# A decode kernel of two attention and two FFN layers: another plan of heads, more held K and V, whole-array zero matmuls

## The chip, the cores and the metric

The kernel runs on one core of a Trainium2 chip. The metric is device time in microseconds (us), the median over executions. The core has five engines with programs of their own: TensorE (PE; weight loads are listed as PEld), VectorE (DVE), ScalarE (ACT), GpSimd (POOL) and SyncE (SP), which here issues all loads. They order their work by semaphores. The load stream runs on 16 DMA engines.

## The reference

Four tokens (batch 4, one position each, D = 448) go through attention, FFN, attention, FFN. Both attention layers use the same weights and the same caches, and both FFNs the same weights.

```python
def _A_ref(x, k_cache, v_cache, wq, wo):      # Hq 16, Hkv 8, Sk 8192, Dh 256
    W = min(4096, max(256, Sk // 4))          # 2048: the last 2048 positions
    q = (x @ wq) ...                          # (4, 16, 1, 256)
    k = jnp.repeat(k_cache[:, :, Sk - W:, :], rep, axis=1)
    v = jnp.repeat(v_cache[:, :, Sk - W:, :], rep, axis=1)
    p = _softmax(einsum("bhqd,bhkd->bhqk", q, k) * (Dh ** -0.5), axis=-1)
    o = einsum("bhqk,bhkd->bhqd", p, v)
    return o ... @ wo
def _B_ref(x, w_gate, w_up, w_down):          # F = 1792
    return (_silu(x @ w_gate) * (x @ w_up)) @ w_down

x = x + _A_ref(_layernorm(x), k_cache, v_cache, wq, wo)
x = x + _B_ref(_layernorm(x), w_gate, w_up, w_down)
x = x + _A_ref(_layernorm(x), k_cache, v_cache, wq, wo)
x = x + _B_ref(_layernorm(x), w_gate, w_up, w_down)
```

For each token, layer and KV head there is a K matrix and a V matrix of 2048 x 256 in bf16, 1 MiB each: 4 x 2 x 8 = 64 uses of a K and 64 of a V. The second layer reads the same matrices as the first.

## The kernel before

**A head** is written as three digits: token, layer, KV head. Head 103 is token 1, layer 0, KV head 3; 113 is the same cache in the second layer. Tokens are independent of one another, so token 0 runs ahead and its second layer overlaps with the first layers of the others. What ties a token's layers together is a chain: the last head of the layer, the output projection, residual, norm, FFN, norm and the new q.

**Buffers.** The tile `half` has 27 slots of 512 KB (NPOOL, HALF). A K or V matrix takes two of them. K is loaded with 16 positions of 256 values per partition, 8 in each half, so that a half has rows of 4 KB. A head of layer 0 that is among the last KEEP_K[t] (or KEEP_V[t]) of its token isn't given back after layer 0: its slots stay taken until layer 1 has used them, and that head isn't loaded again.

**A softmax group** (function `group`) works on one head or on two heads at once ("002+001" in PLAN). Its steps, by line: K half loads (L855), a 32x32 block transpose of each half on DVE (L860), V half loads (L870), the masked query `qe` on POOL (L899), the scores on PE (L894, 32 matmuls of 128 columns for one head and 32 of 256 for two), the row maximum on DVE (L907), its spread over the partitions by two matmuls (L912, L915) and a DVE maximum (L921), exp on ACT (L925), the turn of the probabilities on PE (L938) with a copy on ACT (L947), their sums (L955 on PE, L960 on DVE, the power -1 on POOL, L982), the V product on PE (L969, 8 matmuls for each half), the merge of its two parts (L984 on ACT, L986 on DVE, L992 on PE) and the scaling into `oT` (L1002). Then the output projection adds into the PSUM bank A, as rows (L1022) or, for the heads that end a layer, as columns (L1014). A `stage` of PLAN (a string) is a list of groups whose projections stand together.

**A token's chain**: `rows` (L766, L768, L776, L780) and `residual` (L784) read bank A, `norm` (L551 to L577), then an FFN, `norm` again, and `qproj` (L610 to L646). The FFN exists in two forms: `ffn_row` (L672, tokens in rows, used for the tokens in ROWF) and `ffn` (L726, L753, weights stationary, as many moving columns as there are tokens). A token whose second attention layer is done waits and shares the next token's FFN.

**The order.** Every step is an `Op` in a `Graph`, numbered as it is made. SEQ_PE, SEQ_DVE, SEQ_ACT, SEQ_POOL and SEQ_SP give each engine's program as a list of those numbers, written out by hand of a planner. SLOTS gives the slot of each load in SyncE's order. A load waits until the last PE step that used its slot (`rel`) is done: scores for a K half, the V product for a V half. SyncE issues in order, so a load that waits holds back all behind it. `schedule` estimates start times from each step's duration; they set no order, but which waits can be left out (`_place_waits`).

**Zero matmuls.** In SEQ_PE "w" stands for a matmul of 128 rows and 128 columns of zeros with 512 moving columns into bank A, which adds nothing (L1100), and "q" for the same in four quarters of 32 columns (L1106). 46 are whole, 22 in quarters. `_fill` places waits between them and the steps of other engines on bank A.

Of the kernel before, what the change touches and what calls it, by code (L numbers as in the profile page):

```python
# [20 lines left out]

# [7 lines left out]
FAR_DUR = 0.35  # L29
KEEP_K = (5, 5, 4, 5)  # L30
KEEP_V = (5, 5, 5, 3)


KLEAD = 2.0
KTAIL = 0.1
VLAG = 1.4
SLEAD = -3.4
FR = 8.0
FRD = 9.0
WOR = -5.1  # L40
CROSS = 20
# [4 lines left out]
TRP = 1  # L46
LAND = 1.5
DSTART = 2.1
ROWF = (0, 1)
PLAN = (  # L50
# [4 lines left out]
)  # L55
SEQ_PE = (
# [25 lines left out]
).split()  # L82
SEQ_DVE = (
# [64 lines left out]
).split()  # L148
MMV = 0.034
FAR = 1e30  # L150
FILLD = 0.43
TAIL = {"pe": 0.2, "dve": 0.12, "act": 0.15, "pool": 0.1, "sp": 0.05}

PE, DVE, SCA, POOL, SP = "pe", "dve", "act", "pool", "sp"
# [1022 lines left out]
```

## Time and profile before

| | |
|---|---|
| median of 3 runs | 302.62 us (302.06 to 303.54) |
| span of the profiled execution | 302.5 us |
| read from HBM | 107.58 MB |
| loads: K halves, V halves | 90 and 92 of 512 KB |
| weights: wq, wo, FFN | 3 x 1 MB + 512 KB; 8 x 448 KB; 2 x 1344 KB + 2 x 224 KB + 1568 KB |

The page gives no time of the profiled execution other than its span, from the first to the last instruction. In the profile, busy slices are tenths of 40 equal parts of the span; PEclk is the TensorE clock that was granted, in tenths of full speed. In groups of instructions, "xN" is their count, then busy us in all, mean ns of one, then the idle time of the engine ahead of them and what ended it. Matmuls overlap, so a mean of one is longer than the distance between two. "q" behind an engine's name is its sequencer, which is where loads are issued.

### The profile page before, as it was taken

The numbers are of one execution on the slowest core, as the hardware profiler recorded it, in microseconds if no ns is written. First come the engines' busy times: TensorE is split into PE (matmuls) and PEld (weight loads), VectorE is DVE, ScalarE is ACT, GpSimd is POOL, SyncE is SP. The second block draws the span as 40 slices with busy tenths as digits, with TensorE's granted clock in tenths as the row PEclk, the third lists the DMA queues.
The fourth block names the chain that finished last, engine by engine and source line by source line (L and its number), as shares of the span: only waits on it lengthen the run. The fifth ranks groups of instructions, "written<-read, shape, count | busy, mean of one in ns | idle before, by whom it ended". The sixth has DMA issues, their size and how long they took to land.

```text
span 302.5 us, 11333 instructions
## 1 busy us (share of the span) xinstructions
PE 237.7 (79%) x4962; PEld 140.3 (46%) x4962; DVE 200.8 (66%) x622; ACT 68.7 (23%) x203; POOL 86.3 (29%) x233
## 2 busy tenths in 40 slices
PE   0575598578977887888878869889898898987875
PEld 0322144134433554553445546664565456554554
DVE  7527484428567798966688778788666757675352
ACT  0030011111213323222231323312322121143130
POOL 1521013020412233233323423412126044133232
PEclk9999579855768579657795975855756575589795
DMA  7999999999999999999999999999899997999300
GB/s 284 404 400 400 409 410 404 401 403 402 397 408 384 392 405 408 381 368 401 373 406 403 360 386 366 399 411 353 327 380 395 413 391 303 310 328 408 146 2 3
DMA packets 31921, 108.32 MB, mean 358 GB/s; under 512 B 3192, under 2 KB 7296, under 8 KB 31488
## 3 DMA queue, kind: packets, MB, share of 16 engines
q1 hardware_dynamic: 31872, 107.60, 91.9%
q8 instruction: 39, 0.64, 0.8%
q14 instruction: 10, 0.08, 0.1%
HBM read 107.58 MB, written 0.00 MB: 356 GB/s over the span
## 4 chain that ended last, share of the span: by engine, by line
PE 24%; DMA 15%; DVE 8%; issue 4%; ACT 2%; POOL 0%; SPq 0%
DMA half<-in_A_v_cache_dram 8%; DMA half<-in_A_k_cache_dram 7%; PE Y L969 6%; PE S L894 5%; DVE half L860 3%; PE Z L726 3%; PE Z L753 2%; PE A L1022 2%; PE Y L938 1%; DVE oh L986 1%; PE S L912 1%; PE A L1106 1%; PE A L1014 1%; PE Y L992 1%; PE Y L955 1%
## 5 line engine op out<-in xcount | busy, mean ns | idle before, releaser
L860 DVE STREAM_TRANSPOSE half<-half 128x1024 uint32<-128x1024 uint32 x90 | 110.6, 1235 | 14.7 <-DMA half<-in_A_k_cache_dram 14.2
L969 PE MATMUL Y<-half,pT 128*4 128x256 bf16 (+1 forms) x1024 | 61.3, 341 | 15.6 <-DMA half<-in_A_v_cache_dram 11.6
L982 POOL TENSOR_TENSOR small<-small 128x2 f32<-128x2 f32 (+1 forms) x58 | 42.3, 735 | 74.1 <-DVE small L960 72.7
L894 PE MATMUL S<-half,qe 128*8 128x128 bf16 (+1 forms) x1856 | 53.2, 273 | 6.1 <-DVE half L860 2.7
L894 PEld LDWEIGHTS S<-half,qe 128*8 128x8 bf16 x1856 | 38.8, 102 | 16.1 <-DVE half L860 5.9
L925 ACT ACTIVATE praw<-S,small 104x128 bf16<-104x128 f32 (+1 forms) x58 | 21.8, 376 | 72.0 <-DVE small L921 60.5
L986 DVE SCALAR_TENSOR_TENSOR oh<-oh,small,Y 128x256 bf16<-128x256 bf16 x58 | 27.2, 468 | 14.0 <-ACT oh L984 13.6
L984 ACT ACTIVATE oh<-Y 128x256 bf16<-128x256 f32 x58 | 22.2, 382 | 61.1 <-PE Y L969 43.9
L899 POOL TENSOR_TENSOR qe<-qc,tiny 128x64 bf16<-128x64 bf16 x64 | 18.2, 292 | 62.4 <-PE S L894 50.1
L969 PEld LDWEIGHTS Y<-half,pT 128*4 128x4 bf16 (+1 forms) x1024 | 20.7, 92 | 30.9 <-DMA half<-in_A_v_cache_dram 13.6
L907 DVE TENSOR_REDUCE tiny<-S 104x1 bf16<-104x128 f32 (+1 forms) x58 | 16.8, 292 | 10.0 <-PE S L894 10.0
L947 ACT ACTIVATE pT<-Y 128x64 bf16<-128x64 f32 (+1 forms) x58 | 13.5, 232 | 34.1 <-PE Y L938 27.1
L938 PE MATMUL Y<-sel,praw 104*64 104x32 bf16 x208 | 13.8, 206 | 6.9 <-DVE oT L1002 2.8
L960 DVE TENSOR_REDUCE small<-Y 128x2 f32<-128x32 f32 (+1 forms) x58 | 10.7, 185 | 12.1 <-PE Y L955 11.5
L1002 DVE TENSOR_TENSOR oT<-Y,small 128x4 bf16<-128x4 f32 (+1 forms) x62 | 9.5, 159 | 12.1 <-PE Y L992 5.8
L1022 PE MATMUL A<-wo_sb,oT 128*4 128x448 bf16 x148 | 16.4, 446 | 1.1 <-DVE oT L1002 1.0
L1100 PE MATMUL A<-identb,small 128*128 128x512 bf16 x46 | 16.2, 456 | 0.1
L921 DVE TENSOR_REDUCE small<-S 104x1 f32<-104x32 f32 x58 | 10.3, 181 | 8.2 <-PE S L915 7.9
L912 PE MATMUL S<-small,identb 104*104 104x32 bf16 x58 | 13.5, 235 | 2.8 <-DVE tiny L907 2.6
L992 PE MATMUL Y<-tiny,oh 128*128 128x2 bf16 (+1 forms) x116 | 11.8, 171 | 4.4 <-DVE oh L986 3.9
L992 PEld LDWEIGHTS Y<-tiny,oh 128*128 128x128 bf16 x116 | 7.2, 104 | 15.7 <-DVE oh L986 9.4
L610 PE MATMUL Z<-wq_sb,xn 128*4 128x512 bf16 x120 | 13.9, 601 | 0.8 <-DVE st L563 0.8
(134 smaller groups left out, 276.7 us busy)
## 6 DMA issues: line engine op xcount, KB each, us to landing
half<-in_A_v_cache_dram SPq DMA_DIRECT2D x92, 512.0 KB, 7.8
half<-in_A_k_cache_dram SPq DMA_DIRECT2D x90, 512.0 KB, 7.8
wo_sb<-in_A_wo_dram SPq DMA_DIRECT2D x8, 448.0 KB, 13.7
wq_sb<-in_A_wq_dram SPq DMA_DIRECT2D x3, 1024.0 KB, 7.5
wd_sb<-in_B_w_down_dram SPq DMA_DIRECT2D x1, 1568.0 KB, 20.2
wg_sb<-in_B_w_gate_dram SPq DMA_DIRECT2D x1, 1344.0 KB, 15.9
wu_sb<-in_B_w_up_dram SPq DMA_DIRECT2D x1, 1344.0 KB, 17.2
wq_sb<-in_A_wq_dram SPq DMA_DIRECT2D x1, 512.0 KB, 5.4
```

What stands on the lines that cost most here:

```text
L860: return e.transpose(a, a)
L894: last = e.matmul(Sb[s_][qd:qd + 8, c0:c0 + rhs.free_size()], lhsT=qe[q_][:, P, ce, :, :].rearrange("p a n -> p (a n)"), rhs=rhs, start=(c ...
L899: g.op(POOL, 0.25, pos - SLEAD - 1, lambda e, P=P, t=t, kvh=kvh: e.tensor_tensor(qe[q_][:, P, :, :, :], qc[t][:, kvh, :, :].unsqueeze(2).b ...
L907: g.op(DVE, (0.23, 0.36)[n - 1], pos, lambda e: e.tensor_reduce(pmax[s_][0:R, :], Sb[s_][0:R, 0:N], AX.X, ALU.max), r=(f"s{s_}",), w=(f"pm ...
L925: return e.activation(praw[0:R, 0:128 * n].rearrange("p (g r l) -> p g r l", g=2 * n, l=2), Sb[s_][0:R, 0:128 * n].rearrange("p (l g r) -> ...
L938: last = e.matmul(Yb[p_][64 * h:64 * h + 64, c0:c0 + (48 if n == 2 else 32)], lhsT=praw[0:R, 64 * gg:64 * gg + 64], rhs=w, start=(gg == 0) ...
L969: last = e.matmul(Yb[p_][32 * gg:32 * gg + M, 256:512], lhsT=pT[pt][:, gg, 2 * a + hv, 4 * P:4 * P + M] if n == 2 else p1[:, gg % 2, 2 * a ...
L982: g.op(POOL, 0.69, pos, lambda e: e.tensor_tensor(ri[p_][:, 0:2 * n], rs[p_][:, 0:2 * n], expo[:, 1:1 + 2 * n], op=ALU.pow), r=(f"rs{p_}", ...
L984: g.op(SCA, 0.34, pos, lambda e: e.activation(oh[:, :], Yb[p_][:, 256:512], ACT.Copy), r=(f"y{p_}",), w=("oh",), bank=(f"Y{p_}",))
L986: g.op(DVE, 0.43, pos, lambda e: e.scalar_tensor_tensor(out=oh[:, :], in0=oh[:, :], scalar=lomask[:, 0:1], in1=Yb[p_][:, 256:512], op0=ALU ...
L992: last = e.matmul(Yb[p_][:, 2 * n * dh:2 * n * dh + 2 * n], lhsT=oh[:, :].rearrange("p (m e) -> p e m", e=2)[:, dh, :], rhs=osel[:, 0:2 * ...
L1022: last = e.matmul(Ab[32 * k:32 * k + B, 0:D], lhsT=oT[oi][:, k % 2, k // 2, :], rhs=wo_sb[:, 4 * kvh + k, :], start=False, stop=False, ski ...
```

## The change

Operations of the arithmetic stay as they are; what changes is which heads go together, what is held, how K is loaded, and all orders.

- PLAN has 40 stages with 49 groups in place of 32 with 58: 15 pairs and 34 single heads (6 and 52 before). In six pairs, written with "&", the scores are two steps (`scores(e, Ps)`), one for each head, so that the first doesn't wait for the second K.
- KEEP_K is (6, 5, 4, 7) for (5, 5, 4, 5), KEEP_V (5, 5, 4, 4) for (5, 5, 5, 3): 40 matrices for 37. ROWF is (1, 2) for (0, 1).
- WHOLE names ten heads whose K is one transfer of 1 MB into two neighbouring slots. Heads 315 and 317 in it are held ones, so eight such loads are issued, beside 68 K halves and 92 V halves.
- SyncE's order begins with x, wq and all eight wo, then K; the FFN weights stand in one block behind V of head 007.
- SEQ_PE has 294 whole zero matmuls and none in quarters. "w7" stands between the 6th and the 7th step of other engines on bank A (counted from 0 in the order in which they are made) and waits for the 6th; the 7th waits for the last of them.
- K halves are placed so that their distance in slots never needs two matmuls for one (`keys`).
- In `ffn`, each matmul has its n token columns repeated 32 // n times; the results are read once.
- A PSUM bank's waits go by owner: a step waits for the steps of the engine that had the bank before.
- Step durations come from a table, DUR, and no longer stand in the calls.

```diff
-KEEP_K = (5, 5, 4, 5)
-KEEP_V = (5, 5, 5, 3)
-ROWF = (0, 1)
+KEEP_K = (6, 5, 4, 7)
+KEEP_V = (5, 5, 4, 4)
+ROWF = (1, 2)
 PLAN = (
-    "000", "002+001", "004 005", "006", "003 007", "101", "100 102", "013", "015", "016 106 105", "017", "103",
-    "104 014 107", "201 011 012 202", "010", "200", "116 206 117 207", "114 113 203", "204+115 205", "306", "111 301",
-    "110 112 302", "213 215 305", "303 217+307", "214+304 300", "212", "216 211", "210", "312+314", "315 311",
-    "313+317", "316 310",
+    "000 001", "004 006", "005", "002 003", "007", "101", "100", "102", "014", "013", "016&015", "017+107", "106",
+    "105", "104+103", "012 201+202 011", "204", "010 117+200", "114 113", "115&206", "203", "116", "207+205",
+    "112&111", "110", "302&303", "300 215", "213", "304+216", "307", "306", "301&217", "305", "212", "210",
+    "214 316+314", "311&315", "317+310", "313+211", "312",
 )
+WHOLE = (
+    "000 001 104 111 112 205 207 312 315 317"
+)
...
+            for x in s.split():
+                if x[0] == "w":
+                    o, k = Op(len(self.ops), PE, "fw", filler), max(int(x[1:]), 1)
+                    o.deps[self.writer["identb"]] = True
+                    o.deps[inA[max(k, 1) - 1]] = True
+                    if k < len(inA):
+                        inA[k].deps[o] = True
...
         for b in bank:
-            last = self.banks.setdefault(b, {})
-            for e, d in last.items():
-                if e != eng:
-                    self._dep(o, d, True)
-            last[eng] = o
+            owner, now, before = self.banks.get(b, (eng, [], []))
+            if owner != eng:
+                owner, now, before = eng, [], now
+            for d in before:
+                self._dep(o, d, True)
+            self.banks[b] = (owner, now + [o], before)
...
-                        last = e.matmul((Zb, Z2)[gi][:, n * fc:n * fc + n], lhsT=lhsT, rhs=rhs,
+                        last = e.matmul(block((Zb, Z2)[gi], fc), lhsT=lhsT, rhs=more(rhs),
...
+                    if f"{t}{layer}{kvh}" in WHOLE.split():
+                        g.dma(1 << 20, lambda e, kc=kc, ksrc=ksrc: e.dma_start(
+                            kv[:, HALF * kc[0][0]:HALF * kc[0][0] + 2 * HALF], ksrc[:, :]), None, w=tuple(kk), cells=tuple(kc),
+                            run=8192)
...
+            parts = [(P,) for P in range(n)] if split else [tuple(range(n))]
+            for Ps in parts:
+                kw = dict(acc=(f"s{s_}",)) if Ps[0] else dict(w=(f"s{s_}",))
+                o = g.op(PE, "sch" if split else f"sc{n}", lambda e, Ps=Ps: scores(e, Ps),
+                         r=tuple(k for P in Ps for k in kks[P]) + tuple(f"qe{q_}_{P}" for P in Ps), bank=(f"S{s_}",), **kw)
+                o.rel = tuple(c for P in Ps if free_k[P] for c in kcs[P])
...
+        def filler(e):
+            return e.matmul(Ab[:, 0:512], lhsT=zero[:, 0:1].broadcast_to([128, 128]),
+                            rhs=identb[:, :].unsqueeze(1).broadcast_to([128, 4, 128]), start=False, stop=False,
+                            skip_group_check=True)
```

The new program of TensorE from the first to the second head's projection shows how the zero matmuls stand ("w1" each; sc scores, sp spread, tu turn, to sums, pv V product, fl flip, op projection; the head behind):

```
qsel w1 x38 sc000 w1 x3 sp000 w1 x4 sc001 tu000 w1 to000 sp001 w1 x4 sc004 tu001 pv000 to001 sp004 w1 x2 pv000
sc006 tu004 sp006 to004 fl000 w1 x6 op000 tu006 pv001 sc005 pv001 sp005 to006 w1 x3 fl001 w1 x5 op001 ...
```

More of the change, by code (lines that the diff above doesn't have):

```diff
@@ L172, in __init__ @@
         self.dval = 0
-        self.cell = None
-        self.mate = None
-        self.pairs = ()
-        self.rel = ()
-        self.bank = ()
+        self.cells = self.rel = self.bank = ()
         self.inc = False
@@ L183 @@
 class Graph:
-    filler = None
     tag = None
@@ L240, in _count, with schedule @@
         o.dval = self.dcount[sem]
-    def schedule(self, npool):
-        self.real = len(self.ops)
-        seq = {PE: SEQ_PE, DVE: SEQ_DVE, SCA: SEQ_ACT, POOL: SEQ_POOL, SP: SEQ_SP}
-        order = {e: [self.ops[int(x)] for x in s if x[0] not in "wq"] for e, s in seq.items()}
-        assert sum(map(len, order.values())) == len(self.ops) == len({o for s in order.values() for o in s})
-        loads = [o for o in order[SP] if o.cell is not None]
-        last = {id(c): o for o in self.ops for c in o.rel}
-        held = [None] * npool
-        for o, s in zip(loads, map(int, SLOTS)):
-            o.cell.append(s)
-            self._count(o, f"h{s}")
-            if held[s] is not None:
-                o.deps[last[id(held[s].cell)]] = True
-            held[s] = o
-        for o in self.ops:
-            o.succ = [d for d in o.deps]
+    def schedule(self, npool, filler):
+        real = len(self.ops)
+        inA = [o for o in self.ops if o.eng != PE and "A" in o.bank]
+        order = {}
+        for e, s in ((PE, SEQ_PE), (DVE, SEQ_DVE), (SCA, SEQ_ACT), (POOL, SEQ_POOL), (SP, SEQ_SP)):
+            order[e] = []
+            for x in s.split():
[5 more added lines that the diff above has]
+                        inA[k].deps[o] = True
+                    self.ops.append(o)
+                else:
+                    o = self.ops[int(x)]
+                order[e].append(o)
+        assert sum(map(len, order.values())) == len(self.ops) == len({o.i for s in order.values() for o in s})
+        last = {id(c): o for o in self.ops[:real] for c in o.rel}
+        held = [None] * npool
+        slots = iter(SLOTS.split())
+        for o in order[SP]:
+            if o.cells:
+                s0 = int(next(slots))
+                for s, cell in enumerate(o.cells, s0):
+                    cell.append(s)
+                    if held[s] is not None:
+                        o.deps[last[id(held[s])]] = True
+                    held[s] = cell
+                self._count(o, f"h{s0}")
@@ L259, in schedule @@
         free, at = {e: 0.0 for e in order}, {e: 0 for e in order}
-        done, chan, n = set(), 1.0, 0
+        done, n = set(), 0
         while n < len(self.ops):
-            go = [e for e in order if at[e] < len(order[e]) and all(d in done for d in order[e][at[e]].succ)]
+            go = [e for e in order if at[e] < len(order[e]) and all(d.i in done for d in order[e][at[e]].deps)]
             assert go, "the order does not complete"
@@ L544, in vec @@
-        def vec(rank, emit, r, w, dur=0.16, bank=()):
-            g.op(DVE, dur, rank, emit, r=r, w=w, bank=bank)
-        def norm(t, rank, x):
+                load(3 * 458752, wsb[:, 0:3 * FF].rearrange("p (c n) -> p c n", c=3),
+                     src[0:384, :].rearrange("(c p) n -> p c n", p=128), nm + "a", 3584)
+                load(229376, wsb[:, 3 * FF:], src[384:448, :].rearrange("r (h c) -> (r h) c", h=2), nm + "b", 1792)
+            load(1605632, wd_sb[:, :, :], B_w_down.rearrange("(c p) n -> p c n", p=128), "wd", 896)
@@ L902, in group @@
                     r=(f"qc{t}_{kvh}",) + tuple(f"qmask{a}" for a in range(4)), w=(f"qe{q_}_{P}",))
-            o = g.op(PE, (0.87, 1.72)[n - 1], pos - SLEAD, scores, r=tuple(k for kk in kks for k in kk) + tuple(f"qe{q_}_{P}" for P in range(n)),
-                     w=(f"s{s_}",), bank=(f"S{s_}",))
-            o.rel = tuple(c for kc, fr in zip(kcs, free_k) if fr for c in kc)
-            o.pairs = tuple(kcs)
-            g.op(DVE, (0.23, 0.36)[n - 1], pos, lambda e: e.tensor_reduce(
+            parts = [(P,) for P in range(n)] if split else [tuple(range(n))]
[4 more added lines that the diff above has]
+                o.rel = tuple(c for P in Ps if free_k[P] for c in kcs[P])
+            g.op(DVE, f"max{n}", lambda e: e.tensor_reduce(
                 pmax[s_][0:R, :], Sb[s_][0:R, 0:N], AX.X, ALU.max),
@@ L958, in total @@
                 return last
-            g.op(PE, 0.06 * n, pos, total, r=(f"pT{pt}", "onesb"), w=(f"ysum{p_}",), bank=(f"Y{p_}",))
-            g.op(DVE, 0.2, pos, lambda e: e.tensor_reduce(
+            g.op(PE, f"tot{n}", total, r=(f"pT{pt}", "onesb"), w=(f"ysum{p_}",), bank=(f"Y{p_}",))
+            g.op(DVE, f"sum{n}", lambda e: e.tensor_reduce(
                 rs[p_][:, 0:2 * n].rearrange("p (P n) -> p P n", n=2), sums.rearrange("p k P n -> p P n k"), AX.X, ALU.add),
@@ L1034, in build @@
         gi, oc, waiting, wo_in = 0, 0, [], []
-        for si, heads in enumerate(plan()):
+        for si, (heads, splits) in enumerate(zip(plan(), plan_splits())):
             where = {}
-            for batch in heads:
+            for batch, split in zip(heads, splits):
                 members, outs = [], []
```

474 lines of the change are left out of this document (214 added, 260 removed), and 165 rows, old and new, of tables (SEQ_ACT, SEQ_DVE, SEQ_PE, SEQ_POOL).

## The prediction

> **What bounds the kernel now.** I read the page first, then the busy time by stage, then what the DMA queue waits for, then the chain at the end. The page says that the load stream is the nearest thing to a bound:
>
> ```profile
> span 302.5 us, 11333 instructions
> PE 237.7 (79%) x4962; PEld 140.3 (46%) x4962; DVE 200.8 (66%) x622; ACT 68.7 (23%) x203; POOL 86.3 (29%) x233
> ...
> PEclk9999579855768579657795975855756575589795
> DMA  7999999999999999999999999999899997999300
> ...
> HBM read 107.58 MB, written 0.00 MB: 356 GB/s over the span
> ```
>
> The DMA engines are busy in all but the last three slices, yet TensorE is busy for 79% of the span too, at a granted clock that swings between 0.5 and 1. The stages tell the two apart (columns: window, length, busy us and count of PE, PEld, DVE, ACT, POOL, granted clock, DMA share, GB/s):
>
> ```profile
> 0.00:2.30 2.30, 0.00 (x0) 0.00 (x0) 1.26 (x11) 0.00 (x0) 0.81 (x9) 1.00 0.35 46
> ...
> 12.00:75.00 63.00, 45.04 (x648) 19.66 (x648) 33.80 (x75) 9.68 (x25) 12.12 (x30) 0.79 1.03 403
> 75.00:230.00 155.00, 131.19 (x2906) 80.13 (x2904) 116.46 (x330) 41.43 (x126) 47.96 (x129) 0.71 1.00 385
> 230.00:255.00 25.00, 22.68 (x484) 13.85 (x476) 16.26 (x47) 6.48 (x20) 9.31 (x25) 0.57 1.02 402
> 255.00:282.50 27.50, 22.00 (x547) 13.86 (x548) 17.61 (x56) 6.96 (x20) 8.24 (x22) 0.79 0.89 328
> 282.50:302.50 20.00, 14.71 (x388) 11.16 (x380) 8.12 (x43) 4.19 (x13) 6.05 (x14) 0.70 0.03 9
> ```
>
> 403 GB/s is the rate of a stage in which the queue never runs dry. Against it the middle loses 155 x (1 - 385/403) = 6.9 us and the stage from 255 loses 27.5 x (1 - 328/403) = 5.1 us. So of 302.5 us about 270.5 are bytes at full rate, 12 are stalls of the load stream, and 20 come after the last load. The stalls are waits for buffers, which TensorE frees (the SyncE queue's own waits: who, for whom, us in total, times, longest; last, the K loads' time to landing):
>
> ```profile
> SPq L855 <- PE Y L969: 29.8, 13, 6.9
> SPq L870 <- PE S L894: 17.8, 13, 3.5
> SPq L870 <- PE S L915: 16.5, 8, 4.8
> SPq L870 <- PE Y L992: 14.0, 5, 4.5
> DMA to landing us min/median/max: 3.9/7.8/18.0
> ```
>
> Most of these waits cost nothing, since halves are still queued while SyncE waits (median 7.8 us to landing). A half takes 0.524 MB / 403 GB/s = 1.3 us of transfer; the shortest landing is 3.9 us, so about 2.6 us of it is fixed. A buffer freed more than 2.6 us before the queue runs dry costs nothing.
>
> **The change, part by part.** The sum is made against the profiled execution's own span, 302.5 us; the median of the runs is 302.62, so what lies around the span is taken as 0.1 us.
>
> *Fewer bytes.* The lists KEEP_K and KEEP_V add up to 40 held matrices against 37. 182 halves become 176 (160 half transfers and 8 whole ones), 6 x 0.524 = 3.15 MB less: at 403 GB/s **-7.8 us**. It is nothing if the end is set by TensorE throughout; -8.2 at the 385 of the middle. Six DVE transposes go with it.
>
> *Whole K.* Of the ten names in WHOLE, 315 and 317 are among the seven K held for token 3, so eight transfers with 8-KB rows are issued, not ten. The nearest row is the stretch in which the wq weights, also 8-KB rows, load:
>
> ```profile
> 5.00:10.00 5.00, 0.98 (x7) 0.78 (x7) 4.21 (x38) 0.00 (x0) 0.09 (x1) 1.00 1.02 425
> ```
>
> 8 x 1.05 MB at 425 instead of 403 is -1.1 us; the other bound is 0. One window of weights is thin, and wq3's 4-KB rows are among them, so I take **-0.5**.
>
> *The zero matmuls.* There were 46 whole (L1100) and 22 in quarters (L1106); now 294 whole ones, counted off the order: 45 before the first scores, 64 more up to the scores of head 101, 47 up to token 0's FFN down product, 110 up to the scores of 212, 28 behind. Their price and that of the work around them depends on the clock (timeline: start, length, what, count):
>
> ```profile
> 21.04 0.41 PE L641 MATMUL Z<-wide,identb 128*32 128x128 bf16 x16
> 22.73 0.65 PE L894 MATMUL S<-half,qe 128*8 128x128 bf16 x32 [0.74 <-POOL qe L899]
> 26.58 1.67 PE L1100 MATMUL A<-identb,small 128*128 128x512 bf16 x7
> 33.35 0.60 PE L969 MATMUL Y<-half,pT 128*4 128x256 bf16 x8 [1.95 <-DMA half<-in_A_v_cache_dram]
> 36.64 3.17 PE L1100 MATMUL A<-identb,small 128*128 128x512 bf16 x7
> 61.88 0.54 PE L1022 MATMUL A<-wo_sb,oT 128*4 128x448 bf16 x4
> 70.27 1.02 PE L894 MATMUL S<-half,qe 128*8 128x128 bf16 x32 [0.17 <-DVE half L860]
> 278.27 0.39 PE L969 MATMUL Y<-half,pT 128*4 128x256 bf16 x8
> 282.29 0.36 PE L1022 MATMUL A<-wo_sb,oT 128*4 128x448 bf16 x4
> ```
>
> So a zero matmul costs 1.67/7 = 0.24 us at full clock and 3.17/7 = 0.45 at half; a head's scores 0.65 or 1.02, half a V product 0.39 or 0.60, a row projection 0.36 or 0.54. TensorE runs in program order, so what matters is whether released work stands behind them. In the opening, q is ready at about 21.5 us; 38 zero matmuls put the first scores at 21.5 + 9.1 = 30.6, where before they ran at 22.7. Nothing waits for that: the wo weights now all go ahead of K, and the first K, after 8.4 MB, cannot land before about 24 nor be transposed before 26.5. From there to the scores of 101 there are 64 zero matmuls (15.4 us), eight heads' scores (5.2), eleven V halves (4.3), five projections (1.8) and some thirty small matmuls at 0.2 (6, an estimate; L912 below takes 0.235): 32.7 us, so 63.3. The first load that needs this is the second half of V007, which reuses a buffer that the scores of 101 free, with all FFN weights behind it on SyncE. Up to there 26.7 MB are queued, 68.7 us at 403 GB/s with a start at 2.3 (the first row of the stages); less the 2.6 fixed, the issue must happen by 66.1. There are 3 us to spare at full clock: **+0.5**, and with all of it at half clock 21.5 + 17.1 + 28.8 + 25 = 92.4, 26 us late. Those are the bounds, 0 and +26. I stay near 0 because TensorE has no gap in this stretch, and the clock held in the trace until a gap came (stages of TensorE alone: busy us and count, granted clock, DMA share, GB/s):
>
> ```profile
> 30.00:32.00 2.00, 0.53 (x8) 0.75 1.03 404
> 36.00:38.00 2.00, 1.84 (x8) 0.50 1.05 416
> 40.00:41.00 1.00, 1.00 (x26) 0.50 1.04 414
> 41.00:42.00 1.00, 1.00 (x14) 0.88 1.06 422
> ```
>
> Once it had fallen, at least 5 us of nearly unbroken work, from 36 on, passed before it came back. The Trainium skill (TensorE: Matmul & The Clock Gate, Part 1) says that about 3.4 us of sustained activity suffice. By that rule a fall in the opening would cost some 1.7 us (half of 3.4), by the row 2.5 or more.
>
> *Fewer free buffers at two places.* The KEEP lists leave 27 - 22 = 5 working halves while token 0 is between its layers (7 before) and 5 for token 3 (11 before). Walking SyncE's order beside TensorE's, a buffer is freed with five or fewer unused halves ahead of the queue 31 times (7 before). Around token 0 the loads from 102's V to 106's K each wait for a V product that stands between pieces of the q projection (first a row of the timeline, then the chain of waits at the end: start, length, what):
>
> ```profile
> 87.94 2.73 PE L610 MATMUL Z<-wq_sb,xn 128*4 128x512 bf16 x24
> 288.57 0.32 PE Y L969 x8
> 293.84 3.00 PE Z L726 x112
> 297.42 1.67 PE Z L753 x56
> 300.19 0.61 DVE wo_sb L801
> ```
>
> There I count about 2.3 us lost. Around token 3, between the scores of 210 and the last V product of 214, TensorE has the FFN (3.0 + 1.67, and 0.6 between them by the two starts), a norm (2, my estimate of its part in the 5 us from 288.9 to 293.8), the projection (40 matmuls at 2.73/24 = 4.6) and four V halves (1.6): 13.4 us, in which the order lets about six halves (7.8 us) be issued: 5.6 lost, where the same chain before accounts for the 5.1 from 255 on. The difference is 0.5, with token 0's 2.3 about 3; I take **+3.5**, with bounds 0 (caught up later, where the queue is deep) and +10 (all 7.9 lost on top of the old stall, and 2 more behind it).
>
> *Pairs in place of single heads.* 58 groups become 49 (15 pairs for 6). By form:
>
> ```profile
> L860 DVE STREAM_TRANSPOSE half<-half 128x1024 uint32<-128x1024 uint32 x90 | 110.6, 1235 | 14.7 <-DMA half<-in_A_k_cache_dram 14.2
> L894 PE MATMUL S<-half,qe 128*8 128x128 bf16 x1664 | 44.5, 265 | 5.8 <-DVE half L860 2.4 <-issue 1.9 <-POOL qe L899 1.2
> L986 DVE SCALAR_TENSOR_TENSOR oh<-oh,small,Y 128x256 bf16<-128x256 bf16 x58 | 27.2, 468 | 14.0 <-ACT oh L984 13.6
> L912 PE MATMUL S<-small,identb 104*104 104x32 bf16 x58 | 13.5, 235 | 2.8 <-DVE tiny L907 2.6
> L894 PE MATMUL S<-half,qe 128*8 128x256 bf16 x192 | 8.9, 341 | 0.3 <-DVE half L860 0.3
> ```
>
> Two single scores are 64 x 44.5/1664 = 1.71 us, a pair's 32 x 8.9/192 = 1.48; with one L912 (0.23) a merged pair saves about 0.5 us of PE and at least 0.47 of DVE (L986), nine times 4.4 and 4.2; the transposes are 6 x 1.235 = 7.4 more off DVE. None of that is on the path by itself. Against it stand 110 zero matmuls from token 0's FFN on, 26 us at full clock, 50 at half, where TensorE had 155 - 131 = 24 us idle in the middle: they just fit. If they hold the clock, V products and scores end earlier and buffers come free earlier, and the 6.9 us of stalls in the middle shrink; if not, they stand before released work. Bounds -6.9 and +8; I take **-1.5**, since the orders place few of them in the crowded stages. The FFN products with 32 repeated columns keep their count (112 in 3.00 us, 27 ns each, and the scores' 128 columns take 27 as well: 44.5/1664); the new bank rule and the split scores only move waits: 0.
>
> *The end.* Last load at 282.5, last V product at 288.9, then 13.6 us of row sum, projection, norm, FFN and store. The tail of steps stays. The 6.4 us between were four groups still to be worked off; now the last V belongs to a single head (312), with one pair before it, and the pairs before those have their K held. I take 2.5 for the 6.4: **-4**, bounds -6 and 0.
>
> Sum: 302.5 - 7.8 - 0.5 + 0.5 + 3.5 - 1.5 - 4 = **292.7 us**.
>
> **The rivals.** *TensorE becomes the bound and it gets slower.* The place is the opening; the price is 0.45 for 0.24 us per zero matmul with the work around it; it decides from the moment the scores of 101 come after 66.1 us. With two thirds of the opening at half clock they come at 63.3 + 0.67 x 29.1 = 82.8, 16.5 us late: 292.7 + 16.5 = **309**. For it: the page's clock is 0.5 in many slices where TensorE is busy, and one V half that lands late opens the gap that drops the clock. Against it: the stretch 34 to 42 shows zero matmuls bringing it back. The Trainium skill (TensorE: Matmul & The Clock Gate, Part 3, The mechanism) says that matmuls start and end in strict program order; by that rule any zero matmul ahead of released work is paid in full, which is this rival.
>
> *No gain.* The bytes saved are hidden, because the buffers set the pace: the 7.8 and the 0.5 do not show, the rest of the sum remains: **301**. For it: the four wait rows (78 us) are all for TensorE, and five working halves make them worse. Against: the DMA share is 1.0 up to 255.
>
> *Much better.* The clock is held, no stall in the middle, no loss at tokens 0 and 3, the shortest tail: 302.5 - 7.8 - 1.1 - 6.9 - 6 = **281**. Against it: five working halves.
>
> That the change does not do what it says holds only for the two whole K that are held and never loaded; at 0.14 us each that is no case of its own.
>
> **How the numbers follow.** Forecast 0.50 (its own range 287 to 298), slower 0.22, no gain 0.14, much better 0.14. A measurement of this kernel tells about 0.5% from no change, 301.1 to 304.1. Half of the no-gain case and a small part of the slower one lie in that band: same 0.08, slower 0.21, faster 0.71. The range runs from 282 to 308: about 0.07 lies below and 0.11 above.
>
> **What the profile of after would show.** Bytes: 104.4 MB read. Opening: first scores near 30 us, scores of 101 before 66, granted clock near 1 from 24 to 75, GB/s at 400 up to 85. If the clock is 0.5 there, or GB/s breaks before 75, the slower rival is at work. Tokens 0 and 3: dips of GB/s near 90 and near 245. Middle: fewer slices below 390 GB/s. End: last load near 274 to 279, last V product 2 to 4 us behind its landing, then 13 to 14 us. The forecast is wrong if the load stream ends after 285, or if more than 18 us follow it.

## The result, and the profile after

| | before | after |
|---|---|---|
| time, median | 302.75 us (302.06 to 303.54, 4 runs) | 294.44 us (292.75 to 297.65, 4 runs) |
| ratio to before | | 0.969 (95% interval 0.9646 to 0.9734) |
| profiled execution | span 302.5 us | 294.49 us, span 292.6 us |

1.9 us lie around the span of after. For before I had assumed 0.1, since its profiled execution had no time of its own; in later runs of the same kernel 302.76 us went with a span of 301.0. The profiled execution of before was thus a long one, some 304.3 us (an estimate from these two). By spans the kernel gained 9.9 us, by the medians 8.3. Medians are over all executions; the ratios, here and below, leave out those that took over 1.5% longer than the fastest of the same kernel, so a ratio can differ from that of the medians.

The page of after, beside the first fence of the prediction:

```profile
span 292.6 us, 10922 instructions
PE 251.8 (86%) x4814; PEld 137.6 (47%) x4814; DVE 187.3 (64%) x581; ACT 63.2 (22%) x176; POOL 84.4 (29%) x225
...
PEclk9999999999899797999999979999999995999959
DMA  7999999999999999989999999999999998599500
GB/s 266 401 392 407 410 410 407 408 408 404 391 407 325 381 393 406 408 317 313 413 405 395 417 414 407 407 409 409 403 374 410 409 398 270 212 330 399 230 4 3
...
HBM read 104.44 MB, written 0.00 MB: 357 GB/s over the span
L1084 PE MATMUL A<-identb,small 128*128 128x512 bf16 x294 | 86.0, 394 | 0.7 <-ACT wide L746 0.5
```

TensorE is busier (251.8 us for 237.7), 86.0 of it zero matmuls (L1084), and its clock hardly falls. The stages (columns as in the prediction; the last three are granted clock, DMA share, GB/s):

```profile
12.00:75.00 63.00, 57.76 (x820) 25.11 (x819) 38.56 (x88) 11.18 (x33) 14.59 (x35) 1.00 1.03 405
75.00:120.00 45.00, 40.74 (x804) 23.58 (x803) 22.33 (x66) 8.63 (x25) 12.74 (x35) 0.89 1.01 385
120.00:150.00 30.00, 26.64 (x452) 12.78 (x452) 22.46 (x60) 6.66 (x19) 7.68 (x19) 1.00 0.95 363
150.00:190.00 40.00, 35.00 (x781) 20.73 (x779) 32.13 (x85) 11.39 (x31) 14.83 (x39) 0.96 1.02 408
190.00:230.00 40.00, 34.66 (x727) 18.91 (x721) 30.30 (x86) 11.18 (x29) 13.91 (x38) 1.00 1.01 402
230.00:255.00 25.00, 22.82 (x516) 14.43 (x516) 14.94 (x53) 5.10 (x15) 6.73 (x18) 0.86 0.83 307
255.00:275.00 20.00, 18.30 (x424) 11.08 (x420) 11.23 (x33) 6.76 (x18) 7.55 (x18) 1.00 0.97 369
275.00:292.60 17.60, 13.77 (x313) 9.46 (x309) 6.47 (x37) 2.32 (x7) 3.99 (x11) 0.81 0.02 6
```

Against 403 GB/s the stream loses 45 x (1 - 385/403) = 2.0 us around token 0, 30 x (1 - 363/403) = 3.0 around token 1, and 25 x (1 - 307/403) + 20 x (1 - 369/403) = 6.0 + 1.7 at token 3: 12.7 in all where before lost 12, in other places. Loads end near 275 instead of 282.5, and 17.4 us follow instead of 20. So far that reads as the prediction had it: 6 halves fewer, the same stalls, a shorter end.

Another pair of rows reads differently. A token's new q is finished by the matmuls that turn it (L641 before, L610 after). The rows of tokens 2 and 3, from the timelines of before and of after:

```profile
213.62 0.28 PE L641 MATMUL Z<-wide,identb 128*32 128x32 bf16 x16 [0.28 <-DVE wide L633]
...
266.47 0.28 PE L641 MATMUL Z<-wide,identb 128*32 128x32 bf16 x16
```

```profile
154.24 0.28 PE L610 MATMUL Z<-wide,identb 128*32 128x32 bf16 x16
...
209.43 0.28 PE L610 MATMUL Z<-wide,identb 128*32 128x32 bf16 x16 [0.61 <-DVE wide L602]
...
257.11 0.28 PE L610 MATMUL Z<-wide,identb 128*32 128x32 bf16 x16
```

From token 3's q to the end of the span it is 302.5 - 266.47 = 36.0 us before and 292.6 - 257.11 = 35.5 after. Most of the gain lies ahead of this step: 4.2 us by token 2's q, 9.4 by token 3's. (In two other executions of the old plan, those of e2 and e9 below, token 3's q stands at 263.63 and 265.46 with spans of 302.1 and 302.5, so 9.4 is the upper end of 6.5 to 9.4.) What brought that step forward is what the experiments ask.

### The profile page after: what moved, and what is told of

Read it like the earlier page. It is cut to its first block, busy times and chain, and to the rows that moved or that the text cites. A ratio compares the mean times of both kernels' runs of the same rounds, so it can differ in the third digit from the quotient of the medians.

```text
span 292.6 us, 10922 instructions
## 1 busy us (share of the span) xinstructions
PE 251.8 (86%) x4814; PEld 137.6 (47%) x4814; DVE 187.3 (64%) x581; ACT 63.2 (22%) x176; POOL 84.4 (29%) x225
## 4 chain that ended last, share of the span: by engine, by line
PE 44%; DMA 25%; DVE 18%; issue 5%; SPq 4%; ACT 2%; POOL 1%; DVEq 0%; ACTq 0%
DMA half<-in_A_k_cache_dram 15%; PE A L1084 11%; DMA half<-in_A_v_cache_dram 10%; DVE half L845 9%; PE Y L956 8%; PE S L878 8%; PE Z L705 3%; PE A L1009 2%; SPq L839 2%; DVE oh L973 2%; PE Z L733 2%; PE Z L525 2%; SPq L855 1%; DVE tiny L894 1%; PE S L899 1%
## 5 line engine op out<-in xcount | busy, mean ns | idle before, releaser
L845 DVE STREAM_TRANSPOSE half<-half 128x1024 uint32<-128x1024 uint32 x84 | 102.8, 1232 | 10.6 <-DMA half<-in_A_k_cache_dram 10.3
L1084 PE MATMUL A<-identb,small 128*128 128x512 bf16 x294 | 86.0, 394 | 0.7 <-ACT wide L746 0.5
L956 PE MATMUL Y<-half,pT 128*4 128x256 bf16 (+1 forms) x1024 | 48.6, 283 | 9.2 <-issue 4.0
L878 PE MATMUL S<-half,qe 128*8 128x128 bf16 (+1 forms) x1568 | 46.0, 239 | 4.9 <-issue 2.6
L878 PEld LDWEIGHTS S<-half,qe 128*8 128x8 bf16 x1568 | 30.8, 85 | 17.0 <-DVE half L845 6.6
L1084 PEld LDWEIGHTS A<-identb,small 128*128 128x128 bf16 x294 | 25.4, 101 | 20.0 <-issue 4.1
L973 DVE SCALAR_TENSOR_TENSOR oh<-oh,small,Y 128x256 bf16<-128x256 bf16 x49 | 23.1, 471 | 9.5 <-ACT oh L971 9.1
L541 POOL TENSOR_SCALAR st<-st 128x1 f32<-128x1 f32 x16 | 4.2, 265 | 34.5 <-DVE st L531 32.2
L525 PE MATMUL Z<-st,small 128*128 128x2 f32 x32 | 7.3, 299 | 7.5 <-DVE st L522 7.1
L899 PEld LDWEIGHTS S<-small,identb 104*104 104x104 bf16 x49 | 6.1, 126 | 11.9 <-DVE tiny L894 8.8
## 6 DMA issues: line engine op xcount, KB each, us to landing
wo_sb<-in_A_wo_dram SPq DMA_DIRECT2D x8, 448.0 KB, 11.4
```

The costliest lines, as they stand in the source:

```text
L845: return e.transpose(a, a)
L878: last = e.matmul(Sb[s_][qd:qd + 8, 0:32 * 2 * J], lhsT=qe[q_][:, P, ce, :, :].rearrange("p a n -> p (a n)"), rhs=keys(kcs[P], J * x, J, c ...
L899: e.matmul(Sb[s_][0:R, 256:288], lhsT=identb[0:R, 0:R], rhs=far[0:R, :, :, :].broadcast_to([R, 2, 8, 2]) if n == 2 else far1[0:R, :, :].br ...
L956: last = e.matmul(Yb[p_][32 * gg:32 * gg + M, 256:512], lhsT=pT[pt][:, gg, 2 * a + hv, 4 * P:4 * P + M] if n == 2 else p1[:, gg % 2, 2 * a ...
L973: g.op(DVE, "oho", lambda e: e.scalar_tensor_tensor(out=oh[:, :], in0=oh[:, :], scalar=lomask[:, 0:1], in1=Yb[p_][:, 256:512], op0=ALU.mul ...
L1084: return e.matmul(Ab[:, 0:512], lhsT=zero[:, 0:1].broadcast_to([128, 128]), rhs=identb[:, :].unsqueeze(1).broadcast_to([128, 4, 128]), sta ...
```

## The experiments

Times are medians. Ratios are to the kernel before, run beside it on the same chip; as the runs were spread over several chips and sittings, a difference between two rows is given by the ratios too where it comes out differently.

| run | time, us | ratio (95% interval) |
|---|---|---|
| e1 after, no zero matmuls | 302.28 | 1.0039 (0.9997 to 1.0082) |
| e2 before, no zero matmuls | 303.86 | 0.9957 (0.9897 to 1.0017) |
| e5 after, zero matmuls only up to token 0's FFN | 300.56 | 1.0018 (0.9975 to 1.0061) |
| e6 after, zero matmuls only from there on | 292.78 | 0.973 (0.966 to 0.9799) |
| e7 before, gaps filled with zero matmuls | 306.42 | 1.0201 (1.0127 to 1.0276) |
| e8 after, 2.95 MB fewer | 295.59 | 0.9768 (0.9677 to 0.9859) |
| e9 before, 2.95 MB fewer | 302.59 | 1.0002 (0.9952 to 1.0052) |
| e3 after, no clump at token 1 | 292.23 | 0.9664 (0.9607 to 0.9721) |
| e4 after, no zero matmuls in the tail | 294.56 | 0.9726 (0.9673 to 0.978) |
| e10 after, token 3's loads first | 296.56 | 0.9868 (0.9806 to 0.9931) |
| e11 e6 + e3 + e10 | 296.39 | 0.9854 (0.9794 to 0.9914) |
| e12 e6 + e3 | 292.39 | 0.9664 (0.96 to 0.9728) |

### What are the zero matmuls worth, and where? (e1, e2, e5, e6)

In all four only "w" and "q" entries of SEQ_PE are taken out, as here ahead of the first scores (123):

```diff
-103 w1 w1 104 w1 106
+103 104 106
...
-w1 w1 w1 w1 123 w1 w1 w1 125
+123 125
```

> The kernel after without any of its 294 zero matmuls; everything else in its place. My theory: they are paid for by the clock they hold (0.95 granted in the profile of after against 0.73 before). Without them the clock falls back to about 0.7 and each V product and score takes 0.5 to 1 times as long again, so buffers come free later; the bytes keep their gain. Span 8 us above after's 292.6, time about 301 to 303, which would leave only 0 to 2 us of the whole gain. Rival one: the zero matmuls stand on the chain that ends last with 11% of the span, 32 us, and stand before released work; without them the time falls, to about 288. Rival two: neither; the load stream covers both, and the time stays within 1 us of 294.4 while the clock falls.

> The kernel before without its 46 whole and 22 quartered zero matmuls. With the run without them of the kernel after it separates the plan, the held heads and the orders from the zero matmuls. My theory: 68 of them hold the clock only in the opening, where TensorE has slack, so little changes: 302.7 plus 0 to 3. If the two kernels without zero matmuls then lie about 8 us apart, the plan alone (fewer bytes) brings the gain; if they lie within 2 us, the gain belongs to the zero matmuls. Rival: the clock of the opening decides when the FFN weights are asked for, and without it the time rises by 5 us or more.

> The kernel after with the 156 zero matmuls up to token 0's down product only; the 138 behind it are left out. Without any the time was 302.3 us, with all 294.4, so they are worth 8. Theory: the 8 us come from the middle, where the loads wait for V products and scores at the clock that is granted, and the opening only holds the clock where TensorE has slack. Then this run lies near the one without any: 300 to 302. Rival: the opening sets when the FFN weights are asked for and when token 0's second layer starts, and everything later hangs on that: 295 to 297.

> The kernel after with only the 138 zero matmuls behind token 0's down product; the 156 ahead of it are left out. Theory (the middle earns the 8 us): 294 to 296; the granted clock from 12 to 75 us is lower than 1, and the load stream still holds 403 GB/s there. Rival (the opening earns them): 299 to 302. My prediction gave the opening's zero matmuls a cost of 0.5 us and no gain; by that this run would be 0.5 us below 294.4.

Without zero matmuls the new plan takes 302.28 us: with fewer bytes and fewer groups it is no faster than the kernel before. The 156 up to token 0's FFN down product bring at most 2 of the 8 us (300.56); with only the 138 behind it the time is 292.78, as low as with all. In this last run most of the opening goes at half clock, and the load stream does not notice:

```profile
12.00:75.00 63.00, 36.10 (x653) 19.60 (x653) 37.07 (x78) 10.59 (x30) 13.82 (x33) 0.58 1.03 406
```

How the later ones act shows in the stretch from 155 to 257 us. First the groups of e1, then those of after, then e1's stages:

```profile
L869 PE MATMUL S<-half,qe 128*8 128x128 bf16 (+1 forms) x644 | 25.6, 278 | 3.9 <-DVE half L836 1.8 <-POOL qe L875 0.9 <-DVE oT L980 0.6
L947 PE MATMUL Y<-half,pT 128*4 128x256 bf16 (+1 forms) x424 | 25.2, 336 | 1.2 <-DMA half<-in_A_v_cache_dram 0.8 <-DVE small L938 0.3
```

```profile
L878 PE MATMUL S<-half,qe 128*8 128x128 bf16 (+1 forms) x672 | 21.2, 241 | 2.3 <-issue 1.1 <-DVE half L845 0.6 <-POOL qe L884 0.5
L956 PE MATMUL Y<-half,pT 128*8 128x256 bf16 (+1 forms) x436 | 21.2, 291 | 4.1 <-issue 2.1 <-DMA half<-in_A_v_cache_dram 1.2 <-DVE small L947 0.4
L1084 PE MATMUL A<-identb,small 128*128 128x512 bf16 x62 | 18.6, 385 | 0.0
```

```profile
190.00:230.00 40.00, 34.11 (x649) 19.54 (x650) 27.66 (x83) 9.87 (x25) 13.32 (x38) 0.71 0.96 367
...
255.00:275.00 20.00, 18.13 (x406) 11.77 (x406) 9.16 (x36) 5.65 (x15) 7.32 (x19) 0.83 0.72 267
```

62 zero matmuls stand there in after. With them 672 scores take 21.2 us where 644 took 25.6, and 436 V products 21.2 where 424 took 25.2. That is 8.4 us less of the work that frees buffers; the clock from 190 to 230 is 1.00 for 0.71, and the stream moves 402 GB/s for 367. Token 3's q stands at 263.95 in the profiled execution of e1 (the fastest of its ten) and its span is 299.0: 35.1 us remain, as in after. In e2 the profiled clock was 0.74, as in before; but for one of 298.66, its ten runs lie between 302.0 and 304.9. The zero matmuls of before are worth nothing that can be told.

### Do the bytes count? (e8, e9)

Of six heads the second V half is loaded to one sixteenth; the rest of that half is left out. Each of the six loads still waits for its buffer as before, so only the transfer is shortened. The edit in e8 (the one in e9 does the same):

```diff
+CUT = "103 202 206 111 304 305"
...
-g.dma(1 << 19, lambda e, cell=cell, hv=hv, vsrc=vsrc: e.dma_start(unit(cell), vsrc[hv]), None,
+few = HALF // 16 if hv and f"{t}{layer}{kvh}" in CUT.split() else HALF
+g.dma(1 << 19, lambda e, cell=cell, hv=hv, vsrc=vsrc, few=few: e.dma_start(
+    unit(cell)[:, 0:few], vsrc[hv][:, 0:few]), None,
```

> The kernel after with six V halves (the second of 103, 202, 206, 111, 304 and 305) loaded to one sixteenth, so that 2.95 MB fewer are read; what their V products then compute is not the reference's. Nothing else is changed, neither buffers nor waits. At 403 GB/s these bytes are 7.3 us. Theory (my prediction's: bytes are paid at the full rate wherever the queue isn't dry): 5 to 7.3 us less, 287 to 289.5. Rival (the buffers set the pace, a transfer that ends sooner only waits longer for the next buffer): 0 to 2.5 us less, 292 to 294.5.

> The kernel before with the same six V halves (the second of 103, 202, 206, 111, 304 and 305) loaded to one sixteenth, 2.95 MB fewer; what their V products compute is not the reference's. In the kernel after this cut gave nothing (295.6 against 294.4). My prediction booked fewer bytes at the full rate against the kernel before: 7.3 us less for these, about 295.5. Theory now: the old plan too waits for buffers that TensorE frees at a clock of about 0.7, and transfers that end sooner only wait longer: 0 to 2.5 us less, 300 to 302.5.

Neither kernel got faster. In e8 the stream just runs dry for longer where it did before, and at a new place:

```profile
120.00:150.00 30.00, 26.29 (x430) 12.31 (x426) 21.78 (x57) 5.55 (x15) 6.73 (x19) 0.94 0.89 319
...
190.00:230.00 40.00, 35.79 (x709) 20.08 (x703) 29.22 (x86) 10.54 (x28) 13.94 (x38) 0.91 0.96 366
```

30 x (363 - 319) is 1.3 MB, 40 x (402 - 366) is 1.4 MB: the bytes not read turn up as idle DMA. Token 3's q stands at 256.81, 0.3 us from where it was (from the timeline):

```profile
256.81 0.28 PE L611 MATMUL Z<-wide,identb 128*32 128x32 bf16 x16
```

A DMA share of 1.0 thus did not say that the bytes set the pace: the stream is full because it is as far ahead as the buffers allow. That fewer bytes gave nothing here doesn't say that more would cost nothing. Holding a matrix also removes a wait for a buffer, which these runs keep; whether the new plan needs its 40 held matrices for the zero matmuls to pay wasn't tried.

### Would zero matmuls have done it in the old plan? (e7)

```diff
-51 55 58 65 68 75 w 78 85 w w 97 88
+51 55 58 65 68 75 78 85 w w w w w 97 88
...
```

> The kernel before, with its plan, held heads, transfers and all orders of real work, but with 168 whole zero matmuls in place of its 46 and 22: one for each 0.28 us of the 67 gaps of over 0.3 us that TensorE shows in the run of this kernel without any. Theory one (the plan brings nothing of its own, the gain belongs to the zero matmuls): 295 to 297, as the kernel after. Theory two (both are needed: the clock alone shortens the stalls of the old plan by half, the 3.15 MB fewer bytes the rest): 298 to 300. Rival (the old orders have no room for them, and they stand before released work): 303 or more.

2% slower, with token 3's q at 270.62 in the profiled execution, the longest of the six (310.22 us, the others 305.6 to 307.3). But this isn't the same dose at the same place. Of its 168 only 38 stand between 155 and 270 us (14.5 us), the rest mostly in the opening, and the clock stayed at 0.62 from 190 to 230; after has 62 from 155 to 257. It shows that zero matmuls put into gaps by a rule can cost 4 us by the medians, 6 by the ratio; whether the old plan could gain from well placed ones stays open.

### Single places (e3, e4, e10)

```diff
 e3: between the second and the third V product of the pair 104+103
-604 w6 w6 w6 w6 w6 w6 w6 w6 w6 w6 w6 w6 w6 605
+604 605
 e4: behind the scores of 312, 12 entries
-1592 w30 1587 1615 1594 1595 1618 w31 1620
+1592 1587 1615 1594 1595 1618 1620
```

> The kernel after without the 13 zero matmuls that stand (126.07 to 129.05 us) between token 1's turned row and the V products of the pair 104+103. Behind them stand the scores of 201+202, started at 129.20; their second K half was transposed at 128.29, and SyncE's queue waited 8.12 us from 122.54 for the buffers that these scores free, with 212 GB/s in 130 to 134. My theory: the scores start about 0.9 us earlier, the loads too, and the time falls by 0.5 to 1.5 us, to about 293.5. Rival: a gap of 2 us without matmuls drops the clock to 0.5 and the scores and V products behind take 0.6 to 1.0 us longer, so the time is the same or up to 1 us longer. Second rival: what is won is lost again at token 3, where the queue runs dry anyway, and the time stays within 0.3 us.

> The kernel after without the 12 zero matmuls behind the scores of the last head, 312. On the chain at the end they appear at 279.53, 280.01, 280.86 (two, behind which the residual idled 1.56 us), 282.99, 284.63, 287.01 and 289.19 us. My theory: the clock there was 0.5 from 280 to 285 in spite of them, so they only cost: 1 to 2 us less, about 293. Rival: they bring the clock back in time for the FFN (1.30 and 1.23 us for 42 matmuls, 1.57 for the down product's 56); without them these take up to twice as long, and the time rises by 1 to 3 us.

In e3 both effects that were set against each other came. The stages of e3, then of after:

```profile
126.00:130.00 4.00, 3.40 (x52) 1.72 (x52) 1.44 (x3) 0.38 (x1) 0.54 (x2) 0.50 0.95 372
130.00:134.00 4.00, 4.00 (x68) 2.25 (x70) 3.37 (x11) 1.08 (x3) 0.22 (x2) 0.50 0.96 358
134.00:138.00 4.00, 4.00 (x53) 1.99 (x45) 3.24 (x11) 0.21 (x1) 2.09 (x5) 0.50 0.98 378
138.00:142.00 4.00, 3.88 (x84) 2.32 (x77) 2.54 (x6) 1.18 (x4) 1.03 (x4) 0.91 0.95 317
```

```profile
126.00:130.00 4.00, 4.00 (x58) 2.05 (x54) 2.29 (x3) 0.00 (x0) 0.00 (x0) 1.00 0.91 364
130.00:134.00 4.00, 3.45 (x74) 1.89 (x62) 3.45 (x8) 1.47 (x4) 0.77 (x4) 1.00 0.68 212
```

Without the clump the clock is at half from 126 to 138, and still the stream does not break at 130 (358 GB/s for 212), since the scores behind it stand 2.3 us earlier (126.87 for 129.20) and free their buffers earlier. It breaks later instead: 317 from 138 to 142 for after's 405, and from 120 to 150 it moves 360 for 363. The median is 2.2 us below after's, the intervals overlap; the profiled execution, at 295.25, is one of the two long ones of the six, so whether e3 gains is open. The 12 zero matmuls of the tail are worth nothing either way (294.56).

```diff
 e10, SEQ_PE (1468 scores of 214, 1384 FFN down, 1450 sums and 1452, 1453 V products of 210, 1391 norm)
-1432 w28 w28 1384 1434 1448 1468 1391 1450 1470 1394 1400 1401 1403 1404 1452 1453 1473
+1432 1468 1384 1434 1448 1450 1452 1453 1391 1470 1394 1400 1401 1403 1404 1473
 SEQ_DVE: 1464 moved ahead of 1381, 1469 ahead of 1388, 1451 ahead of 1393
```

> The kernel after with another order around token 3's chain: the scores of 214 stand ahead of the FFN's down product (the two zero matmuls there go), the V products of 210 ahead of norm and q projection, and on VectorE the transpose of 214's second K half ahead of the FFN's elementwise steps. In the profile of after the loads of V halves wait for these scores until 252.4 us and for these V products until 255.3, and 250 to 255 moves only 127 GB/s. Theory (five working halves make these steps set the end): the loads go out about 3 us earlier, 250 to 255 moves 250 GB/s or more, and the time falls by 1.5 to 3 us, to 291.5 to 293. Rival (the end hangs on token 3's chain of norm, FFN and q, which gets 0.5 to 1 us later): same or up to 1 us slower, though the dip is filled.

2 us slower by the medians, 5 by the ratios, against the theory. The timeline of e10 around the step:

```profile
246.92 0.65 PE L878 MATMUL S<-half,qe 128*8 128x128 bf16 x32
...
251.40 0.35 PE L1009 MATMUL A<-wo_sb,oT 128*4 128x448 bf16 x1 [2.00 <-issue]
...
254.14 1.45 PE L579 MATMUL Z<-wq_sb,xn 128*4 128x512 bf16 x12
...
258.92 0.28 PE L610 MATMUL Z<-wide,identb 128*32 128x32 bf16 x16
```

and of after:

```profile
250.40 0.56 PE L878 MATMUL S<-half,qe 128*8 128x128 bf16 x25
252.10 0.28 PE L878 MATMUL S<-half,qe 128*8 128x128 bf16 x7 [1.14 <-issue]
...
253.20 0.82 PE L579 MATMUL Z<-wq_sb,xn 128*4 128x512 bf16 x12
```

The stages from 250 on, of e10 and of after:

```profile
250.00:255.00 5.00, 2.71 (x39) 1.39 (x43) 0.74 (x5) 0.59 (x2) 1.19 (x4) 0.89 0.74 237
255.00:260.00 5.00, 4.46 (x73) 1.75 (x69) 1.04 (x5) 1.76 (x4) 1.29 (x5) 0.77 0.54 170
```

```profile
250.00:255.00 5.00, 3.77 (x83) 2.09 (x86) 1.63 (x14) 0.59 (x2) 1.96 (x6) 1.00 0.39 127
255.00:260.00 5.00, 4.29 (x115) 2.87 (x109) 1.81 (x7) 2.04 (x5) 2.17 (x8) 1.00 1.00 356
```

The scores of 214 did start 3.5 us earlier (246.92 for 250.40), and 250 to 255 moves 237 GB/s for 127; what was won there is missing right behind it (170 for 356). A stop of 2.00 us fell ahead of the moved V products, the first part of the q projection took 1.45 us for 0.82, and token 3's q came 1.8 us later. From there to the end it is 295.1 - 258.92 = 36.2 us. This speaks for token 3's chain as what sets the end, and against the dip in the load stream beside it: the rival had the mechanism and at most half of the size. How much of the 1.8 us is the order's own doing isn't shown. The norm's first matmuls (L525) start 0.9 us later (253.25 for 252.31), and the stop ahead of them was 0.9 us longer (2.00 for 1.14); the other 0.9 is the projection at a lower clock.

### Together (e11, e12)

> Three edits of the kernel after together: no zero matmuls ahead of token 0's down product (alone 292.8), none of the 13 of token 1's clump (alone 292.2), and token 3's order as in the run beside it. If they add up: 294.4 - 1.7 - 2.2 - 2 = 288.5. If they are all paid for at one place (the load stream runs dry at token 3 whatever comes before), the sum is that of the last alone: 291 to 293. Rival: without the opening's zero matmuls and the clump the clock stays at 0.5 longer behind token 0, and the time is 294 or more.

> The kernel after with two edits that each went with a lower time alone: no zero matmuls ahead of token 0's down product (292.8) and none of the 13 of token 1's clump (292.2); token 3's order stays as it was. If they add up: 294.4 - 1.7 - 2.2 = 290.5. If both only bring the same stretch forward, up to the place where token 3 makes the load stream run dry: 292 to 293. Rival (with fewer zero matmuls ahead, the clock is at 0.5 for longer between token 0 and token 1 and the stalls there grow): 294 or more.

They don't add. e11 is as slow as e10 alone, e12 (292.39) no faster than e3 or e6 alone. e12's median is 2 us below after's, but 0.9664 (0.96 to 0.9728) and 0.969 (0.9646 to 0.9734) can't be told apart. No version was found that surely beats the kernel after.

## Why the prediction came out, by its own steps

The forecast of 292.7 us was 1.7 below the measured 294.44, and by spans it said -9.8 where -9.9 came. The sum came out right by luck: two wrong terms cancelled.

- **Fewer bytes, -7.8: failed.** "At 403 GB/s" took a full queue for a binding one. 2.95 MB fewer are worth nothing in either kernel (1.0002 in before), and the plan with 3.15 MB fewer but no zero matmuls is at 302.28. The reason of the no-gain rival (buffers set the pace) was the right one; its time of 301 is close to that of e1 and e5. The wait rows spoke for it with 78 us, and I set the DMA share of 1.0 against them.
- **Pairs and the clock in the middle, -1.5: mis-sized.** By the medians the zero matmuls behind token 0's FFN are worth 300.56 - 294.44 = 6.1 (e5, after) to 302.28 - 292.78 = 9.5 us (e1, e6), at or past the bound of -6.9; by the ratios it is 9.9 and 9.3. The mechanism named there (they hold the clock, scores and V products end earlier, buffers come free earlier) is what the groups of e1 and after show. I held it small by counting the 6.9 us of stalls as all there was to win; but where the cycle of buffers sets the pace, shorter work brings the whole chain forward. That is my reading of these rows; no run took the clock apart from the zero matmuls.
- **Opening, +0.5: held.** Scores of the first head ran at 28.36 us (30.6 forecast), those of 101 at 60.76 (63.3), 405 GB/s up to 75, the clock at 1.00. Without those 156 the time is 292.78, not told apart. The slower rival (309, zero matmuls and the work around them at half clock in the opening) did not come up. In e6 the clock is at 0.58 from 12 to 75 and it cost nothing, but there the zero matmuls are missing too, so this shows only that the work alone has room at half clock; the rival's price was not tested.
- **Fewer free buffers, +3.5: places right, meaning wrong.** 2.0 us are missing around token 0 (2.3 forecast) and 7.7 at token 3 (5.6); the 3.0 at token 1 I had not seen. But such a stall is not a term of the sum: filling one (e3, e10) emptied another behind it.
- **The end, -4: mis-sized.** 17.4 us follow the last load for 20, -2.6.
- **Whole K, -0.5: not tried by itself;** it is below what these runs can tell.
- **Around the span, 0.1: wrong,** 1.8. By it alone 292.7 becomes 294.5. But the same error hid that the span I started from belonged to an execution some 1.6 us longer than the median: against the medians I forecast a gain of 9.9 us where 8.3 came.

What stays open is how much of the gain needs the new plan: e1 shows that the plan alone gives nothing, e7 does not show that zero matmuls alone could not.

## What to carry to other kernels

Before booking bytes at the full rate, shorten a few transfers and see whether the end moves: a full DMA queue also occurs where the release of buffers sets the pace. Look for a step from which the variants need about the same time to the end (here token 3's q: 34.9 to 36.8 us in after and its variants); what did not bring that step forward gained nothing there, however good the stage looked. It is a guide and no law: in the old plan the rest is 36.0 to 38.5 us, and in e2 this q came 2.8 us earlier than in before while the span fell by 0.4. Zero matmuls pay where TensorE's real work frees buffers, and only a run without them, stage by stage, tells which ones do.

## What the runs showed of the hardware that I had not expected

**TensorE stops at a place of its program, not at an operation.** The stop of 1.14 us in after falls inside the scores of 214, the one of 2.00 us in e10 inside a projection. Up to it both have run the same number of matmuls; the stretches from 0 to the stop, of after and of e10:

```profile
0.00:250.96 250.96, 216.95 (x4044) 115.55 (x4045) 168.56 (x506) 53.77 (x151) 71.01 (x192) 0.96 0.99 387
```

```profile
0.00:249.39 249.39, 216.25 (x4044) 114.98 (x4044) 168.31 (x502) 53.44 (x150) 71.07 (x191) 0.97 1.00 390
```

In the stretch from 249 to 252.2 after's DMA queues show one packet of code:

```profile
q8 instruction: 1, 0.02, 1.7%
```

The packet moved between 249 and 250, ahead of the stop. Other stops of 0.4 us or more in after for which the profile shows no releaser stand behind 1234, 1489, 2511 and 3533 matmuls (1.48, 1.86, 1.48 and 0.63 us). From each of the five to the next it is 255, 1022, 1022 and 511 matmuls: 2, 8, 8 and 4 times about 127.75, which with as many weight loads makes 255.5 instructions. The whole program has 4814 / 127.75 = 37.7 such pieces, and this queue brought 38 packets; without the zero matmuls (e1) it is 4520 / 127.75 = 35.4 and 35. In e6, where 156 matmuls fewer stand ahead of every later step, the stops lie at other steps, but behind 2127, 2255, 3150, 3278 and 4299 matmuls, on the same grid. So the place is a matter of TensorE's program and not of the step that stands there. How long a stop lasts differs from execution to execution: behind 1489 matmuls it was 1.86 us in after and 2.98 in e10.

I take these stops for the loading of TensorE's program; no run tried what sets their length. The Trainium skill (Runtime: NRT & Kernel Launch, Instruction fetch mechanics) says that engines fetch code in blocks of 16 KiB, 256 instructions, and that crossing into the next is mostly hidden. The packets agree in size and the distances in count; the 1.14 and 2.00 us are not hidden.

**The clock came back late.** In e3 it stayed at 0.50 from 126 to 138 us although TensorE was busy for 11.4 of those 12 us, and was at 0.91 only after 138. The Trainium skill (TensorE: Matmul & The Clock Gate, Part 1) says that about 3.4 us of sustained activity bring full speed; this row needed more than three times that, and more than the 5 us on which the prediction counted. Why is open.

**The recorded clock is not always the clock.** The profile of e1 gives a clock of 1.00 from 12 to 75 us, where that of e6, with the same program up to there, gives 0.58. But the 352 matmuls of scores take 304 ns each in e1 and 303 in e6, against 218 in after: both went at half clock, and the record of e1 is wrong there. The mean clocks of e1's ten executions, 0.70 to 0.85, can't be compared for that reason. The stretches used above agree with the durations in them.
